# Gate and value weights of batch 0 as 16-bit parts, seven products for eight in batch 1, two score rows in one run

## The chip, the core and the metric

The kernel runs on one core of a Trainium2 chip. The metric is the time on the device in microseconds, the median of several executions. Before the change it is 1017.41 us (three executions, 1014.47 to 1018.92).

## What is computed

Three blocks in a row, with 4 batches (B), 8 heads, 576 tokens (S), head width 64. The first is causal attention plus a read of a memory, mixed by a gate for each head; the other two are feed-forward blocks. The reference, cut to the sums that matter:

```python
scores = scale * np.matmul(q, k.transpose(0, 1, 3, 2))      # then causal mask, softmax -> a
local = np.matmul(a, v)
x = g * mem_out + (1 - g) * local                            # [2304, 512]
h = (x @ w1) * (x @ w2) @ w3                                 # 512 -> 1024 -> 1024
x2 = h @ w_out                                               # 1024 -> 512
gate = 1.0 / (1.0 + np.exp(-(x2 @ w_gate)))                  # 512 -> 1536
out = gate * (x2 @ w_val) @ w_out2                           # 1536 -> 512
```

## The kernel before

**Precision.** Every product of two 32-bit matrices is made from parts: each operand is split into a high and a low part, and three matmuls (high by high, low by high, high by low) add up in PSUM (`prod`, L519). The parts are either 32-bit words of a reduced format ("fp32r" in the profile) or 16-bit words (f16). For f16 the operand is first scaled by a power of two, taken from its largest entry (`power`, L158: four one-column steps on VectorE behind a small matmul, `total`, L168, that spreads a column's sum to all partitions).

**Stages.** `ffn(b)` (L757) runs the two feed-forward blocks of batch b in four stages, with names as in the trace: `ab` (x by w1 and w2, 8 column blocks f), `xw` (h by w3 and w_out multiplied together beforehand, 4 blocks d; its result is x2), `gv` (x2 by the gate and value weights, 12 blocks f) and `ot` (by the last matrix). The matmuls have 288 columns: half of the 576 tokens (hf = 0, 1). `drive` (L1381) slips the steps of the next batch's attention in between, at the places where `ffn` yields: in ab, xw and ot, not in gv. So gv is a stage of matmuls in a row.

**Eight or seven products.** `gv` and `ab` need the products of a 2 by 2 block matrix with a 2 by 2 block matrix. In batches 0 and 1 all eight are made: 48 matmuls for a block f of gv. In batches 2 and 3 `two_rows` (L580) makes seven from sums and differences of blocks, 42 matmuls for each f, with more work behind them: adds of 288 columns on VectorE and one on GpSimd for each f. It needs the weight blocks in two forms, plain parts ("P") and parts of sums ("S", made by `sums`, L431: four adds of 256 columns on VectorE), and seven operands of x2 instead of four (`token_steps`, L546).

**Weights.** They come as 64-bit words in DRAM. `conv_step` (L379) turns half a unit (one f of gate and value is one unit, 8 blocks of 128) into 32-bit floats with two ACT steps and one DVE step, takes its largest entry (`mcol`) and stores the whole unit (`kept`). In batch 0 `split_step` (L458) then splits each half into fp32r parts, one ACT and one DVE step of 512 columns for each half, into a ring of 5 slots (`wslot`). `pump` (L489), called after each second product, does one step of each of these. The 16-bit parts are made later, by a list of tasks (`late_split`, L321): load the kept unit, split it on ACT and DVE (1024 columns), store it. A table `PACE` says at which pumps a task step comes, `limit` how far the list may go.

**Order of work.** TensorE runs in the order in which the code is written. The order on the other engines is fixed when the kernel is built, and every engine takes its instructions in that order, each waiting for its inputs. Three PSUM buffers, `f`, go round for the products and for `total`; two, `s`, hold scores. For a row block i of the scores of a head pair p, `s_part` (L1146) makes six matmuls (three for each head) and two masked reductions on DVE, which write the tiles `p`.

## Time and profile before

| what | value |
|---|---|
| median of three executions | 1017.41 us (1014.47 to 1018.92) |
| the profiled execution | 1013.13 us |
| its span in the trace | 1011.3 us |
| TensorE matmuls (PE) busy | 982.4 us, 97% |
| weight loads (PEld) busy | 797.9 us, 79% |
| VectorE (DVE) busy | 731.3 us, 72% |
| ScalarE (ACT) busy | 596.6 us, 59% |
| GpSimd (POOL) busy | 195.0 us, 19% |
| granted TensorE clock, mean | 0.995 of full speed |

The stages of the trace, found from the first and last matmul of each name: batch 0 has ab at 118 to 219 us (with the last of w3 by w_out between), xw to 257.3, gv to 334.1, ot to 385.7; batch 1 ab to 466.6, xw to 499.5, gv to 570.1, ot to 622.1; batch 2 ab to 681.5, xw to 721.3, gv to 786.0, ot to 845.0; batch 3 ab to 886.6, xw to 912.5, gv to 976.3. A busy share over the whole span says little here, since the stages differ; the table of stretches below is the one to read.

### The profile page before, as it was taken

Reading aid. Unit: us, or ns where it says so; the run is one execution under the profiler, and the core shown is the slowest. Engines: PE = TensorE matmul, PEld = TensorE weight load, DVE = VectorE, ACT = ScalarE, POOL = GpSimd, SP = SyncE. Lnnn points to the kernel's source line nnn. Section 1 sums busy time; section 2 is a strip of 40 time slices with the busy share of each in tenths; the row PEclk is TensorE's granted clock in tenths of the full one; section 3 lists DMA queues with packets and bytes.
Section 4 is the critical chain, followed back from the end, with each engine's and each line's share of the span. In section 5 each row is a group of like instructions: output and inputs, shape, how many; then the busy total and the mean of one; then the engine's idle time right before and its main releaser. Section 6 shows DMA issues by size and latency. Waiting matters only on the chain. (4 is left out here: it accounts for less than half of the span.)

```text
span 1011.3 us, 19894 instructions
## 1 busy us (share of the span) xinstructions
PE 982.4 (97%) x7351; PEld 797.9 (79%) x7351; DVE 731.3 (72%) x1702; ACT 596.6 (59%) x1213; POOL 195.0 (19%) x196
## 2 busy tenths in 40 slices
PE   7999999999999999999999999999999999999998
PEld 3556687888999898898977777778777667797776
DVE  6866788777778826777777668988876757737883
ACT  7987787567777735564654545555655545324451
POOL 3454012213000101312200011343111311201110
PEclk9989999999999999999999999999999999999999
DMA  8865799967777249877887576655655556556532
GB/s 293 245 230 192 247 346 310 326 206 254 249 250 247 98 137 380 286 226 238 297 310 261 176 251 240 214 190 184 200 181 178 185 157 204 186 174 246 183 131 79
DMA packets 95642, 227.21 MB, mean 225 GB/s; under 512 B 11192, under 2 KB 39992, under 8 KB 95288
## 3 DMA queue, kind: packets, MB, share of 16 engines
q1 hardware_dynamic: 95544, 225.93, 66.3%
q8 instruction: 58, 0.95, 0.4%
q14 instruction: 40, 0.33, 0.1%
HBM read 164.55 MB, written 61.34 MB: 223 GB/s over the span
## 5 line engine op out<-in xcount | busy, mean ns | idle before, releaser
L532 PEld LDWEIGHTS <-wslot 128*128 128x128 f16 x1680 | 162.9, 98 | 49.7 <-issue 8.3
L1200 POOL TENSOR_SCALAR p<-p,sm,omg 116x116 f32<-116x116 f32 (+4 forms) x100 | 89.0, 895 | 406.2 <-DVE sm L1198 294.9
L521 PE MATMUL gv<-x,wslot 128*128 128x288 f32 (+1 forms) x1152 | 147.5, 290 | 0.2 <-ACT gsb L137 0.2
L521 PEld LDWEIGHTS <-wslot 128*128 128x128 f16 x1152 | 111.1, 98 | 32.1 <-issue 4.5
L532 PE MATMUL gvp<-x,wslot 128*128 128x288 f16 x1008 | 125.2, 286 | 3.6 <-ACT x L180 1.6
L137 ACT ACTIVATE p<-p,sm 116x116 f32<-116x116 f32 (+4 forms) x160 | 93.2, 585 | 46.6 <-DVE sm L1174 46.5
L521 PE MATMUL ot<-hg,wslot 128*128 128x288 f16 (+1 forms) x864 | 118.1, 291 | 0.0
L521 PE MATMUL ab<-x,wslot 128*128 128x288 f32 x768 | 117.2, 302 | 0.5 <-ACT asb L800 0.3
L521 PE MATMUL xw<-h,wslot 128*128 128x288 f32 x768 | 113.0, 300 | 1.7 <-ACT h L721 1.0
L521 PEld LDWEIGHTS ab<-x,wslot 128*128 128x128 f32 x768 | 104.0, 188 | 6.3 <-issue 2.9
L521 PEld LDWEIGHTS xw<-h,wslot 128*128 128x128 f32 x768 | 103.4, 188 | 5.5 <-issue 2.0
L1174 DVE CUSTOM_DVE_ANT_0 p<-s,msk 116x116 f32<-116x116 f32 (+4 forms) x160 | 68.0, 452 | 30.8 <-PE s L1169 26.8
L532 PE MATMUL abp<-x,wslot 128*128 128x288 f16 x672 | 87.1, 286 | 1.3 <-DVE u2ab L603 1.1
L723 DVE TENSOR_TENSOR wslot<-wraw,wslot 128x512 fp32r<-128x512 f32 x76 | 54.9, 725 | 34.7 <-ACT wslot L721 34.4
L521 PEld LDWEIGHTS gv<-x,wslot 128*128 128x128 f32 x576 | 76.4, 188 | 0.5 <-ACT gsb L137 0.5
L1230 PE MATMUL t<-idf,p 116*116 116x116 f32 x480 | 68.7, 272 | 3.3 <-DVE p L1200 2.5
L1230 PEld LDWEIGHTS t<-idf,p 116*116 116x116 f32 x480 | 54.3, 139 | 18.0 <-issue 5.3
L402 ACT ACTIVATE cy<-r 128x512 f32<-128x512 f32 x76 | 51.5, 678 | 13.3 <-DVE wraw L411 2.6
L721 ACT CAST wslot<-wraw 128x512 fp32r<-128x512 f32 x76 | 47.1, 621 | 16.2 <-PE gv L521 7.4
L411 DVE SCALAR_TENSOR_TENSOR wraw<-cy,cr 128x512 int32<-128x512 int32 x76 | 54.2, 740 | 2.6 <-ACT cr L403 2.1
L521 PE MATMUL wps<-wo,wslot 128*128 128x512 f32 x192 | 52.2, 407 | 0.0
L1248 ACT COPY pt<-t 116x696 f32<-116x696 f32 (+2 forms) x74 | 47.5, 650 | 7.4 <-PE t L1230 7.1
(210 smaller groups left out, 1630.0 us busy)
## 6 DMA issues: line engine op xcount, KB each, us to landing
wslot<-k SPq DMA_DIRECT2D x40, 512.0 KB, 4.3
wslot<-ka SPq DMA_DIRECT2D x40, 512.0 KB, 4.4
wrawl<-kf SPq DMA_DIRECT2D x32, 512.0 KB, 6.1
wslot<-kb SPq DMA_DIRECT2D x40, 384.0 KB, 3.5
k<-wslot SPq DMA_DIRECT2D x24, 512.0 KB, 4.7
r<-in_gv_dram SPq DMA_DIRECT2D x24, 512.0 KB, 5.1
...
```

The costliest lines, as they stand in the source:

```text
L137: ins = nc.scalar.activation(**kw)
L402: nc.scalar.activation(out=y, in_=hi, func=AF.Prelu, scale=2.0**-112, alpha=2.0**32)
L411: nc.vector.scalar_tensor_tensor(z, y, 3, tmp["r"], ALU.logical_shift_left, ALU.bitwise_or)
L521: paced["pe"] = nc.tensor.matmul(ps, w[:, wi, blk, :], x[:, xi, cols : cols + n], start=first and part == 0, stop=last and part == 2,)
L532: paced["pe"] = nc.tensor.matmul(ps, w[:, wi, blk + k, :], x[:, xi, k, :], start=not more and k == 0 and part == 0, stop=k == 1 and part == 2,
L721: nc.scalar.copy(dst[:, 0], src)
L723: eng.tensor_sub(dst[:, 1], src, dst[:, 0].bitcast(F32))
L1174: nc.vector.tensor_tensor_reduce(out=ps_[hh][:, c0:c1], in0=os_[hh], in1=msk[:, SP - w + c0 : SP - w + c1], scale=-0.125, scalar=3.0e38 if ...
L1200: lower(SHARE_N).tensor_scalar(ps_[hh][:, :w], ps_[hh][:, :w], sm[:, 6 + hh : 7 + hh], omg[:T, 2 * p + hh : 2 * p + hh + 1], ALU.mult, ALU ...
L1230: nc.tensor.transpose(tp[:T, c : c + T], src[hh][:, j * T : (j + 1) * T], idf[:T, :T])
L1248: nc.scalar.copy(to, got)
```

## The change

In batch 0 the gate and value units are split into f16 parts at once. `scaled_step` waits until both halves of a unit are converted, makes the unit's scale (`unit_scale`: two one-column matmuls, four one-column DVE steps), splits the whole unit in one ACT and one DVE step of 1024 columns and stores the result, which batches 1 to 3 load as their "P" form. So x2 of batch 0 has to be f16 and scaled as well: its bound needs the largest entry of each h block (`htop`, 8 DVE reductions of 576 columns more) and of the product matrix (`wmax`, moved ahead into xw), and each f gets its own factor to scale back.

In batch 1 gv takes the path of batches 2 and 3 (`two_rows`, seven products), and x2 of batch 1 their `token_steps`. The task list loses its 12 "P" tasks for gate and value, and their 12 "S" tasks come first, from batch 0's ot on; the P and S tasks of a and b come after them, the S tasks of the last matrix may now run from batch 2's ab on. `PACE` is set anew.

For batches 1 to 3 the scores of row blocks 0 and 1 are made in one run of twelve matmuls, into the two `s` buffers side by side. The `p` tiles get 6 buffers instead of 5, the loads of q one instead of two.

```diff
-PB = 5
+PB = 6
-PACE = (4, 4, 4, 14, 4, 8, 4)
+PACE = (2, 9, 3, 14, 8, 5, 8)
...
-    tasks = [(u, "P") for u in jobs[:F2]] + [(("o", *x), "P") for x in pairs_of]
+    tasks = [(u, "S") for u in jobs[:F2]] + [(("o", *x), "P") for x in pairs_of]
     NFIRST = len(tasks)
     tasks += [(u, "PS") for u in jobs[F2:]]
     NPARTS = len(tasks)
-    tasks += [(u, "S") for u in jobs[:F2]]
-    NSUMS = len(tasks)
     tasks += [(("o", *x), "S") for x in pairs_of]
...
-    again = plain["ab"] + plain["xw"] + gv8 + ot8
+    again = plain["ab"] + plain["xw"] + gv16 + ot8
...
+    def unit_scale(u):
+        n = rank[u]
+        power(wsc[:, n : n + 1], wsc[:, NJ + n : NJ + n + 1], total(f"wsum{n}", *(mcol[:, hf, n : n + 1] for hf in range(2))))
+        scaled.add(u)
+    def scaled_step(u, now):
+        if ws["conv"] < 2 * u + 2:
+            return False
+        if u not in scaled:
+            if not now and ws["pumps"] < ws["ready"]:
+                return False
+            unit_scale(u)
+            return True
+        if in_use("wslot") >= RING:
+            return False
+        w = fp.tile([128, 2, 8, 128], F16, tag="wslot", name=f"wslot{ws['ring']}", bufs=RING)
+        split_scaled(w[:, 0], w[:, 1], raws.pop(u), wsc[:, rank[u] : rank[u] + 1])
+        nc.sync.dma_start(out=whole16[u]["P"], in_=w)
+        done.append((u, "P"))
+        put("wslot", [w])
+        ws["split"] += 2
+        return True
...
         if b == 2:
-            ws["pace"] = PACE[3]
+            ws["limit"], ws["pace"] = len(tasks), PACE[3]
...
-            if b > 0:
-                largest(htop[:, f : f + 1], hraw, AX.X)
+            largest(htop[:, f : f + 1], hraw, AX.X)
...
+                if b == 0 and d == 0 and n == 1:
+                    while ws["tops"] < KC:
+                        assert conv_step() or split_step()
+                    nc.vector.tensor_reduce(wmax, wtop.rearrange("p d f -> p f d"), AX.X, ALU.max)
+                    x2s = bound_x2(b, htop)
...
-            if b == 2:
+            if b:
                 for _ in two_rows(
                     take(2), x2, f"gv{b}_{f}", hraw[:, :HS], hraw[:, HS:], x2back[:, f : f + 1], True
                 ):
...
-            s = take(1 if b else 2)
+            s = take(1)
+            slot(s)
+            nc.vector.tensor_mul(x2back[:, f : f + 1], wsc[:, NJ + f : NJ + f + 1], x2s[:, 1:2])
...
         if b == 0:
             late_scales()
-            ws["limit"], ws["pace"] = F2, PACE[0]
+            ws["limit"], ws["pace"] = NFIRST, PACE[0]
...
         def s_part(p, i, n):
+            if i == 1 and not first:
+                return
+            rows = (0, 1) if i == 0 and not first else (i,)
...
+            for i, w, c0, c1, at in jobs:
+                for x, (q_, k_) in enumerate(terms):
+                    for hh in range(2):
+                        r = slice(64 * hh, 64 * hh + 64)
+                        nc.tensor.matmul(
+                            os_[hh][:, at : at + c1 - c0], q_[r, 0, i * T : (i + 1) * T], k_[r, 1, c0:c1],
+                            start=x == 0, stop=x == len(terms) - 1,
+                        )
```

How the order of instructions moves, at three places. The first is VectorE in the gv loop of batch 0, where `hgraw` is gate times value of one f, `gv0_f_hf_w` the product it reads from PSUM, `wraw` a unit being converted, `mcol` its largest entry, `wslot` its parts, and `hg` the low part of the result. Before, one whole round:

```order
L411 SCALAR_TENSOR_TENSOR wraw29_3323<-cy58_3305,cr58_3306 128x512
L411 SCALAR_TENSOR_TENSOR wraw29_3323<-cy59_3335,cr59_3336 128x512
L723 TENSOR_TENSOR wslot46_3326<-wraw27_3147,wslot46_3326 128x512
L176 TENSOR_REDUCE mcol_86<-wraw29_3323 128x1
L723 TENSOR_TENSOR hg0_0_3234<-hgraw0_0_3235,hg0_0_3234 128x576
L176 TENSOR_REDUCE mcol_86<-wraw29_3323 128x1
L964 TENSOR_TENSOR hgraw0_1_3315<-gv0_1_0_1_3343,gsb0_1_0_3341 128x288
L723 TENSOR_TENSOR wslot47_3382<-wraw27_3147,wslot47_3382 128x512
L964 TENSOR_TENSOR hgraw0_1_3315<-gv0_1_1_1_3375,gsb0_1_1_3373 128x288
```

After, half a round, from the last multiply of one f to the first of the next:

```order
L969 SCALAR_TENSOR_TENSOR hgraw0_2_3484<-gv0_2_1_1_3556,x2back0_2897,gsb0_2_1_3554 128x288
L163 TENSOR_SCALAR pw_3549<-wsum6_3546 128x1
L953 TENSOR_TENSOR x2back0_2897<-wsc_83,x2s0_2813 128x1
L164 TENSOR_SCALAR wsc_83<-pw_3549 128x1
L181 SCALAR_TENSOR_TENSOR wslot45_3530<-wraw29_3295,wsc_83,wslot45_3530 128x1024
L165 TENSOR_SCALAR pw_3549<-wsc_83 128x1
L746 TENSOR_TENSOR hg0_2_3483<-hgraw0_2_3484,hg0_2_3483 128x576
L436 SCALAR_TENSOR_TENSOR wraw32_3563<-cy64_3540,cr64_3541 128x512
L166 TENSOR_SCALAR wsc_83<-pw_3549 128x1
L436 SCALAR_TENSOR_TENSOR wraw32_3563<-cy65_3576,cr65_3577 128x512
L181 SCALAR_TENSOR_TENSOR wslot46_3566<-wraw30_3402,wsc_83,wslot46_3566 128x1024
L969 SCALAR_TENSOR_TENSOR hgraw0_3_3586<-gv0_3_0_1_3612,x2back0_2897,gsb0_3_0_3610 128x288
```

The two splits of 512 columns in each round are gone; there are splits of a whole unit (1024 columns, `wsc` is the scale) and the one-column steps of `power` (L163 to L166) and of the factor `x2back`, two units close together in every other round.

The second place is TensorE in the ab stage of batch 1, with scores of batch 2's pair 1 (`s2_1_i`). Before, row block 0, and some 40 matmuls later row block 1:

```order
L1169 MATMUL s2_1_0_0_0_5250<-qkh2_1_5194 116x116
L1169 MATMUL s2_1_0_0_1_5251<-qkh2_1_5194 116x116
L1169 MATMUL s2_1_0_0_0_5250<-qkh2_1_5194,qkl2_1_5195 116x116
L1169 MATMUL s2_1_0_0_1_5251<-qkh2_1_5194,qkl2_1_5195 116x116
L1169 MATMUL s2_1_0_0_0_5250<-qkl2_1_5195,qkh2_1_5194 116x116
L1169 MATMUL s2_1_0_0_1_5251<-qkl2_1_5195,qkh2_1_5194 116x116
L521 MATMUL ab1_3_0_1_5240<-x1_2_4327,wslot83_5064 128x288 x3
```

```order
L1169 MATMUL s2_1_1_0_0_5321<-qkh2_1_5194 116x232
L1169 MATMUL s2_1_1_0_1_5322<-qkh2_1_5194 116x232
L1169 MATMUL s2_1_1_0_0_5321<-qkh2_1_5194,qkl2_1_5195 116x232
L1169 MATMUL s2_1_1_0_1_5322<-qkh2_1_5194,qkl2_1_5195 116x232
L1169 MATMUL s2_1_1_0_0_5321<-qkl2_1_5195,qkh2_1_5194 116x232
L1169 MATMUL s2_1_1_0_1_5322<-qkl2_1_5195,qkh2_1_5194 116x232
L521 MATMUL ab1_3_1_1_5309<-x1_2_4327,wslot83_5064 128x288 x3
```

After, both stand in one run:

```order
L1181 MATMUL s2_1_1_0_0_5368<-qkh2_1_5309 116x116
L1181 MATMUL s2_1_1_0_1_5369<-qkh2_1_5309 116x116
L1181 MATMUL s2_1_1_0_0_5368<-qkh2_1_5309,qkl2_1_5310 116x116
L1181 MATMUL s2_1_1_0_1_5369<-qkh2_1_5309,qkl2_1_5310 116x116
L1181 MATMUL s2_1_1_0_0_5368<-qkl2_1_5310,qkh2_1_5309 116x116
L1181 MATMUL s2_1_1_0_1_5369<-qkl2_1_5310,qkh2_1_5309 116x116
L1181 MATMUL s2_1_1_0_0_5368<-qkh2_1_5309 116x232
L1181 MATMUL s2_1_1_0_1_5369<-qkh2_1_5309 116x232
L1181 MATMUL s2_1_1_0_0_5368<-qkh2_1_5309,qkl2_1_5310 116x232
L1181 MATMUL s2_1_1_0_1_5369<-qkh2_1_5309,qkl2_1_5310 116x232
L1181 MATMUL s2_1_1_0_0_5368<-qkl2_1_5310,qkh2_1_5309 116x232
L1181 MATMUL s2_1_1_0_1_5369<-qkl2_1_5310,qkh2_1_5309 116x232
```

One run of scores amid the products is gone for each pair of heads.

The third place is VectorE in the gv loop of batch 1, which now has the seven products (`gvp`) with their sums `u2`, `u3`. After:

```order
L631 TENSOR_TENSOR u2gv1_4_6813<-gvp1_4_6_6806,s1gv1_4_6804 128x288
L181 SCALAR_TENSOR_TENSOR wP18_6830<-wrawl_18_6534,wsc_83,wP18_6830 128x768
L181 SCALAR_TENSOR_TENSOR hg1_3_6712<-hgraw1_3_6713,hgs1_6698,hg1_3_6712 128x576
L648 TENSOR_TENSOR u3gv1_4_6842<-gvp1_4_6_6806,s1gv1_4_6804 128x288
L652 TENSOR_TENSOR u2gv1_4_6813<-gvp1_4_5_6815,u2gv1_4_6813 128x288
L659 TENSOR_TENSOR u3gv1_4_6842<-u3gv1_4_6842,gvp1_4_4_6853 128x288
L622 SCALAR_TENSOR_TENSOR hgraw1_4_6794<-s5gv1_4_6822,x2back1_6143,u2gv1_4_6813 128x288
L622 SCALAR_TENSOR_TENSOR hgraw1_4_6794<-u3gv1_4_6842,x2back1_6143,c11gv1_4_6834 128x288
L631 TENSOR_TENSOR u2gv1_5_6887<-gvp1_5_6_6880,s1gv1_5_6878 128x288
L181 SCALAR_TENSOR_TENSOR hg1_4_6793<-hgraw1_4_6794,hgs1_6698,hg1_4_6793 128x576
```

A split of a task (`wP18`, 768 columns, of a and b) stands between the adds that free PSUM buffers; 16 instructions of tasks stand in this stage in all, 8 splits and 8 adds of 256 columns, and in that of batch 2 before the change there were 5.

## Rows read from the trace of the kernel before

**Rows 1.** The page, busy time of each engine with its share of the span.

```profile
PE 982.4 (97%) x7351; PEld 797.9 (79%) x7351; DVE 731.3 (72%) x1702; ACT 596.6 (59%) x1213; POOL 195.0 (19%) x196
```

**Rows 2.** Stretches: PE, PEld, DVE, ACT, POOL busy (instructions), clock, DMA.

```profile
118.00:219.00 101.00, 97.89 (x698) 83.33 (x697) 80.23 (x189) 69.72 (x152) 18.05 (x17) 1.00 0.88 307
219.00:257.30 38.30, 36.64 (x285) 32.59 (x284) 30.66 (x75) 26.79 (x58) 9.86 (x8) 1.00 0.75 261
257.30:334.10 76.80, 76.56 (x578) 76.26 (x578) 60.36 (x108) 58.25 (x110) 0.00 (x0) 1.00 0.72 244
...
499.50:570.10 70.60, 70.60 (x580) 56.40 (x579) 51.95 (x90) 39.23 (x55) 0.00 (x0) 1.00 0.80 270
...
622.10:681.50 59.40, 58.17 (x480) 43.25 (x478) 52.96 (x147) 34.18 (x85) 24.31 (x23) 1.00 0.69 225
...
721.30:786.00 64.70, 62.59 (x507) 49.30 (x506) 49.65 (x103) 33.97 (x64) 9.41 (x12) 1.00 0.57 192
786.00:845.00 59.00, 56.75 (x465) 41.09 (x464) 43.07 (x108) 32.18 (x61) 10.30 (x10) 1.00 0.51 163
...
912.50:976.30 63.80, 62.33 (x507) 49.24 (x506) 48.97 (x103) 31.45 (x63) 9.40 (x12) 1.00 0.56 195
```

**Rows 3.** PE in order of time, gate and value products of batch 0.

```profile
262.42 71.82 PE L521 MATMUL gv<-x,wslot 128*128 128x288 f32 x540 [0.24 <-ACT gsb L137]
334.09 0.21 PE L172 MATMUL wsum<-mcol,ones 128*128 128x20 bf16 x2
334.15 1.85 PE L521 MATMUL ot<-hg,wslot 128*128 128x288 f32 x12
```

**Rows 4.** PE in order of time, the same products in batches 1 and 2.

```profile
517.18 53.08 PE L521 MATMUL gv<-x,wslot 128*128 128x288 f16 x432
...
743.41 42.79 PE L532 MATMUL gvp<-x,wslot 128*128 128x288 f16 x348 [0.31 <-ACT s5gv L608]
```

**Rows 5.** DVE in order of time, one round of batch 0's gate and value loop.

```profile
283.42 0.45 DVE L964 TENSOR_TENSOR hgraw<-gv,gsb 128x288 f32<-128x288 f32 x1
283.79 1.28 DVE L411 SCALAR_TENSOR_TENSOR wraw<-cy,cr 128x512 int32<-128x512 int32 x2
284.99 0.68 DVE L723 TENSOR_TENSOR wslot<-wraw,wslot 128x512 fp32r<-128x512 f32 x1
285.59 0.68 DVE L176 TENSOR_REDUCE mcol<-wraw 128x1 bf16<-128x512 f32 x1
286.19 0.75 DVE L723 TENSOR_TENSOR hg<-hgraw,hg 128x576 fp32r<-128x576 f32 x1
286.86 0.68 DVE L176 TENSOR_REDUCE mcol<-wraw 128x1 bf16<-128x512 f32 x1
287.45 0.45 DVE L964 TENSOR_TENSOR hgraw<-gv,gsb 128x288 f32<-128x288 f32 x1
289.17 0.69 DVE L723 TENSOR_TENSOR wslot<-wraw,wslot 128x512 fp32r<-128x512 f32 x1 [1.27 <-ACT wslot L721]
289.78 0.45 DVE L964 TENSOR_TENSOR hgraw<-gv,gsb 128x288 f32<-128x288 f32 x1
```

**Rows 6.** PE in order of time, a run of scores amid batch 1's products.

```profile
410.83 5.41 PE L521 MATMUL ab<-x,wslot 128*128 128x288 f32 x39
416.17 0.31 PE L1169 MATMUL s<-qkh 64*116 64x116 f32 x2
...
416.62 0.66 PE L521 MATMUL ab<-x,wslot 128*128 128x288 f32 x3
417.11 0.76 PE L1230 MATMUL t<-idf,p 116*116 116x116 f32 x6
```

**Rows 7.** Groups by shape: busy us, mean ns | idle before, releaser.

```profile
L176 DVE TENSOR_REDUCE htop<-hraw 128x1 f32<-128x576 f32 x24 | 17.9, 747 | 0.4
...
L181 DVE SCALAR_TENSOR_TENSOR wP<-wrawl,wsc,wP 128x1024 f16<-128x1024 f32 x12 | 15.7, 1305 | 11.6 <-ACT wP L180 11.0 <-DMA wslot<-k 0.5
...
L1198 DVE RECIPROCAL sm<-sm 116x2 f32<-116x2 f32 x80 | 12.8, 160 | 1.3
```

More of the change, by code (lines that the diff above doesn't have):

```diff
@@ L271, in tile_attention_memory_ffn @@
     wot = {}
-    ws = {"conv": 0, "step": 0, "split": 0, "ring": 0, "freed": 0, "use": 0, "again": 0, "pumps": 0, "late": 0, "task": 0, "part": 0, "limit": 0, "pace": 0, "tops": 0, "wo": 0, "pass": 0, "wready": False}
+    ws = {"conv": 0, "step": 0, "split": 0, "ring": 0, "freed": 0, "use": 0, "again": 0, "pumps": 0, "late": 0, "task": 0, "part": 0, "limit": 0, "pace": 0, "ready": 0, "tops": 0, "wo": 0, "pass": 0, "wready": False}
     tmp = {}
+    scaled = set()
     last = {}
@@ L327, in late_split @@
         late_o2 = u not in rank
+        if late_o2 and "o2" not in scaled:
+            scaled.add("o2")
+            o2_scale()
+            return
         by = o2s[:, 0:1] if late_o2 else wsc[:, rank[u] : rank[u] + 1]
@@ L464, in split_step @@
         u, hf = divmod(s, 2)
+        if u in rank and rank[u] < F2:
+            return scaled_step(u, now)
         r = raws[u][:, 4 * hf : 4 * hf + 4, :]
@@ L870, in measure @@
         def measure(f):
[L871 to L877 removed]
+            if f == 0:
                 for n, m in enumerate((0, 1, 5, 4)):
@@ L1173, in s_part @@
[L1173 to L1183 removed]
+            if i == 1 and not first:
+                return
@@ new lines, in s_part @@
+            rows = (0, 1) if i == 0 and not first else (i,)
+            jobs = []
+            at = 0
+            for i in rows:
+                w = T * (i + 1)
+                if n == 0:
+                    ps_ = []
+                    for hh in range(2):
+                        name = f"p{b}_{p}_{i}_{hh}"
+                        if first and np_["n"] % 2 == 0:
+                            m = np_["n"] // 2 % P0
+                            ps_.append(fp.tile([T, 2 * S], F32, tag=f"h{m}", name=name, bufs=1)[:, :SP])
+                        else:
+                            ps_.append(ap.tile([T, SP], F32, tag="p", name=name, bufs=PB))
+                        np_["n"] += 1
+                    sp[p, i] = (ps_, ap.tile([T, 8], F32, tag="sm", name=f"sm{b}_{p}_{i}", bufs=6))
+                c0, c1 = (0, w) if w <= 512 else ((0, SP // 2), (SP // 2, SP))[n]
+                jobs.append((i, w, c0, c1, at))
+                at += c1 - c0
@@ new lines, in s_part @@
+            os_ = [
+                ps_s.tile([128, 512], F32, tag="s", name=f"s{b}_{p}_{i}_{n}_{hh}")[:T, :at] for hh in range(2)
+            ]
+            terms = [(qks[p], qks[p])] if first else [(parts[p][x], parts[p][y]) for x, y in ((0, 0), (1, 0), (0, 1))]
+            for i, w, c0, c1, at in jobs:
+                for x, (q_, k_) in enumerate(terms):
+                    for hh in range(2):
+                        r = slice(64 * hh, 64 * hh + 64)
+                        nc.tensor.matmul(
+                            os_[hh][:, at : at + c1 - c0], q_[r, 0, i * T : (i + 1) * T], k_[r, 1, c0:c1],
+                            start=x == 0, stop=x == len(terms) - 1,
+                        )
```

133 lines of the change are left out of this document (39 added, 94 removed).

## The prediction

> **What bounds the kernel now.** I read the page first: matmuls keep TensorE busy for 982.4 us of the span [rows 1], so the kernel ends when TensorE has done its list, and the change is worth what it takes off that list, less the new waits. A share over the whole span hides the stages, so the table of stretches came next [rows 2]. In gv of batch 0 TensorE is busy 76.56 of 76.80 us and weight loads 76.26; in gv of batch 1, with f16 parts, 70.60 of 70.60 and loads 56.40. Neither has waits worth naming: only a shorter list helps. VectorE is the engine to watch, since the new work lands on it: 60.36 of 76.80 there, and 52.96 of 59.40 in ab of batch 2, the fullest stretch shown. Then TensorE in order of time gave the price of one product [rows 3, 4, 6], and VectorE in order of time the room that is left in a round [rows 5]. The granted clock is 1.00 in all these stretches, the 2.4 GHz level.
>
> The profiled execution took 1013.13 us with a span of 1011.3; the median shown is 1017.41, 4.3 us more. I make the sum as a difference and take it off the median.
>
> **Gate and value of batch 0.** 540 fp32r matmuls take 71.82 us, 133.0 ns each [rows 3]; f16 ones 53.08 us for 432, 122.9 ns [rows 4]. For 576 that is 10.1 ns x 576 = 5.8 us off. Added are 24 one-column matmuls in 12 pairs; the nearest row is `wsum`, a pair after which the next product starts 0.06 us later [rows 3]: 12 x 0.06 = 0.7 us, if their operands are there. They are: by the order, each unit's `mcol` steps stand well ahead of its pair.
>
> What can spoil this is VectorE. Its round for one f takes 6.36 us now (283.42 to 289.78), of which it sits idle 1.27 us for ScalarE's part of the split [rows 5]. By starts, two conversions take 1.20 us, a largest entry 0.60, `hg` 0.67, a multiply 0.37 to 0.45. After: two conversions 1.20, two largest 1.20, one split of 1024 columns 1.22 (the row has 1.305 [rows 7]; neighbours overlap by about 0.08), two multiplies 0.88, `hg` 0.67, and five one-column steps, which no row shows alone: between 0.04 and 0.16 us each (the two-column reciprocal [rows 7]); I take 0.1, since other steps stand between them. Sum 5.7 us, from 5.4 to 6.0. TensorE's round becomes 48 x 0.1229 + 0.06 = 5.96 us. So VectorE just keeps up on average, but not evenly: the order puts two splits, two conversions, `hg` and the small steps between one multiply and the next, 5.3 us, while TensorE makes the next product in 24 x 0.1229 = 2.95 us. The multiply then comes 2.3 us late, and what waits behind it is the product that needs its PSUM buffer: with three buffers about 2.95 us of lateness cost nothing, with a `total` in between about half. I take 2.0 us of waits over the 8 or 9 full rounds; the ends are 0 and the case where the idle 1.27 us stays in each round (second rival). Another 0.3 us goes where gv begins, since the last split of x2 stands behind conversions and unit splits; the ends are 0 and the 1.66 us that TensorE now idles in xw (38.30 less 36.64 [rows 2]). Net gain 5.8 - 0.7 - 0.3 - 2.0 = **2.8 us**.
>
> ScalarE costs nothing: 24 casts of 512 columns become 12 of 1024, and it is busy 58.25 of 76.80 us [rows 2]. Of the DMAs, the 12 late loads and 12 late stores of the P tasks go, and 12 stores come into gv. Such a store waits in SyncE's queue for its split, and behind it stand the loads of the next raw halves; these run three halves ahead, a round and a half or 8.9 us, which covers it. Without that cover conversion would wait, as in the second rival.
>
> **Gate and value of batch 1.** The stage takes 70.60 us; the same stage with seven products takes 64.70 in batch 2 and 63.80 in batch 3 [rows 2]. These hold the waits at the start for the seven operands, the GpSimd adds and the extra DVE work; the products run at 42.79 us for 348, 123.0 ns [rows 4]. But batch 1 also has tasks in it: 16 VectorE instructions, some 13 us (8 splits at 1.0 to 1.3 us, 8 short adds at about 0.44), against 5 of some 3 us in batch 2. VectorE would be busy 49.65 + 10 = 60 of 65 us. The nearest row for that is ab of batch 2, 52.96 of 59.40 us with the same seven products and tasks, where TensorE idles 1.23 us [rows 2]. I take 64.70 + 1.6 = 66.3: gain **4.3 us**, from 6.8 (as batch 3) to -4 (each task's work exposed).
>
> The Trainium skill, "Perfetto Trace Analysis", section "Identifying the Most-Contended Engine", says that matmul busy time does not tell how far TensorE is from its limit, that the busy share of LDWEIGHTS does, and that for VectorE occupancy is a fair measure. By it TensorE would have room in f16 stages (loads busy 56.40 of 70.60 us), and ab of batch 2 would be VectorE's stage (89% against 73%). The trace does not agree: TensorE idles there 1.23 us in 59.40, and f16 products come every 122.9 ns however busy the loads are. By the page the stage limit of gv in both batches would be VectorE's load, about 60 us and with the waits the second rival's time.
>
> **Scores.** Twelve runs go (three batches, four pairs). Three ab matmuls after a run take 0.49 us to the next foreign matmul; at the rate of the long stretch, 5.34 us for 39, they would take 0.41 [rows 6]. So a break costs about 0.1 us on entering, and the run of six (0.45 us) holds about as much for leaving. One break less: 0.15 us x 12 = **1.8 us**, from 1.0 to 2.4. The same reductions stand on VectorE, and both `s` buffers stay taken a little longer; row block 2's scores come later than either.
>
> **Tasks moved.** In ot of batch 2 TensorE idles 59.00 - 56.75 = 2.25 us and VectorE is busy 43.07 us with the last tasks in it [rows 2]; the order has none there after. Gain **1.0 us**, from 0 to 2.25. Five or six of them now lie in gv of batch 2: loss 0.5 us, up to 1.5.
>
> **Costs elsewhere.** Eight largest entries of h at 0.747 us [rows 7] are 6.0 us more on VectorE in ab of batch 0, where it is busy 80.23 of 101 us and TensorE idles 3.1 [rows 2]: 1.0 us more idle (0 to 3). The last of them stands ahead of the last split of h, for which TensorE already waits: 0.7 us. In batch 1's ab the S tasks come at every fifth pump: 0.5 us; in ot of batch 0, where they replace the P tasks, 0.2. Together with 0.5 above: **2.9 us**.
>
> **Sum.** 2.8 + 4.3 + 1.8 + 1.0 - 2.9 = 7.0 us. 1017.4 - 7.0 = **1010.4 us**, 0.7% less.
>
> **Rivals.**
> First, everything is hidden: VectorE keeps up in both gv stages. Then 5.8 - 0.7 = 5.1 from batch 0, 6.8 from batch 1, 2.4 from scores, 1.5 from ot and no costs: 15.8 us, 1001.6. For it: TensorE hardly waits at 89% VectorE load [rows 2]. Against: the uneven order in batch 0.
>
> Second, slower: VectorE and ScalarE wait for each other in gv of batch 0 as they do now, and the 1.27 us stay [rows 5]. The round becomes 6.0 + 1.27 = 7.3 us instead of 6.36, and nine rounds lose 8.5 us instead of gaining 2.8: 1010.4 + 11.3 = 1021.7. The whole change turns slower than before where the round passes 6.36 + (7.0 - 2.8) / 9 = 6.8 us, that is with 1.1 us of idle time in a round of 5.7. Against it: the split now waits for a scale made pumps earlier and is needed later, as a slot holds a whole unit and five units fit the ring instead of two and a half.
>
> Third, batch 1's tasks are exposed: the splits stand between the adds that free PSUM buffers, and 10 us more VectorE work lengthen the stage to 74.7 us: 4.1 lost instead of 4.3 won, 1018.8. Half of it gives 1014.6. For it: products of 0.74 us and three buffers leave little room. Against: ab of batch 2.
>
> Fourth, the order on the engines as built differs in stages that the edits don't name, and eats the gain: 1015.
>
> **Chances.** Forecast 0.52 (1006 to 1014.5), first rival 0.20, second 0.09, third 0.13, fourth 0.06. The range leaves out the lower half of the first rival and most of the second: **1001.5 to 1018.5**. About 0.5%, 5.1 us, is what a measurement of this kernel can tell from no change. Faster by more (under 1012.3): 0.42 of the forecast, all of the first, little else: 0.62. Slower by more (over 1022.5): half of the second and a little of the third: 0.08. Within: 0.30.
>
> **What would show it.** In the trace after: gv of batch 0 in about 73.5 us with products 122.9 ns apart, and TensorE's waits there naming `hgraw` or `wsum`; gv of batch 1 in about 66.3 us; 24 `wsum` matmuls without waits; VectorE idle in ot of batch 2; one run of twelve score matmuls in each pair. The prediction is wrong if VectorE's round in batch 0's gv takes over 6.4 us, if gv of batch 1 takes over 68 us, or if TensorE's idle time grows by more than 3 us in ab of batch 0.

## The result and the profile after

The changed kernel takes **1029.29 us** (median of four executions, 1026.71 to 1032.05), against 1016.28 before (four executions): a ratio of 1.0133, with a 95% interval of 1.0098 to 1.0168. It is 13 us slower where 7 us less were forecast. The profiled execution took 1032.05 us with a span of 1030.3, 18.9 more than that of before, so a sum over stages of the two traces comes to more than the medians' 13: the traced execution of before is one of the fast ones of its kernel, the one after the slowest of four.

The page after, busy time of each engine, to be held against [rows 1]:

```profile
PE 976.5 (95%) x7303; PEld 776.8 (75%) x7303; DVE 763.0 (74%) x1804; ACT 597.9 (58%) x1220; POOL 207.5 (20%) x208
```

TensorE's list did get shorter, by 5.9 us of busy time, yet the span is 19 us longer. So it waits more: span less busy time was 28.9 us and is 53.8. Where, the table of stretches after tells, with the columns of [rows 2]: ab, xw and gv of batch 0, ab and gv of batch 1, ab, gv and ot of batch 2.

```profile
119.50:228.90 109.40, 100.15 (x698) 85.61 (x697) 84.02 (x190) 69.60 (x151) 17.64 (x15) 0.97 0.81 282
228.90:271.50 42.60, 39.48 (x290) 35.05 (x291) 35.07 (x98) 29.25 (x59) 9.48 (x8) 0.92 0.75 264
271.50:347.90 76.40, 72.03 (x597) 56.80 (x595) 67.33 (x147) 60.91 (x102) 0.00 (x0) 1.00 0.87 318
...
397.30:484.50 87.20, 81.49 (x624) 71.94 (x624) 74.04 (x186) 46.56 (x106) 21.32 (x20) 0.96 0.72 248
...
518.00:585.30 67.30, 63.06 (x508) 49.20 (x505) 56.71 (x113) 38.58 (x71) 10.51 (x12) 1.00 0.83 284
...
637.20:701.30 64.10, 58.75 (x481) 43.34 (x480) 56.95 (x147) 35.36 (x87) 24.36 (x23) 1.00 0.61 199
...
741.80:807.10 65.30, 62.82 (x508) 49.37 (x508) 52.92 (x112) 35.06 (x66) 10.16 (x12) 1.00 0.60 193
807.10:864.40 57.30, 55.51 (x464) 40.94 (x462) 27.89 (x79) 27.14 (x56) 10.23 (x9) 1.00 0.27 79
```

The stages that the change rewrites, gv of batch 0 and 1 and ot of batch 2, are shorter. The loss lies in ab of batch 0 (+8.4), xw of batch 0 (+4.1), ab of batch 1 (+6.4) and ab of batch 2 (+4.6). In three of the four the granted clock is below 1.00, where it was 1.00 before. The row of before for ab of batch 1:

```profile
385.70:466.60 80.90, 80.19 (x626) 70.32 (x625) 59.98 (x160) 48.97 (x108) 22.12 (x20) 1.00 0.81 283
```

TensorE in order of time, the longest waits in ab and xw of batch 0 and ab of batch 1 after the change:

```profile
129.46 1.41 PE L1244 MATMUL t<-idf,p 116*116 116x116 f32 x6 [2.74 <-DVE p L1214]
160.09 0.61 PE L1244 MATMUL t<-idf,p 116*116 116x116 f32 x2 [3.32 <-DVE p L1214]
205.52 0.38 PE L1244 MATMUL t<-idf,p 116*116 116x116 f32 x2 [2.19 <-DVE p L1214]
234.45 0.53 PE L549 MATMUL xw<-h,wslot 128*128 128x288 f32 x2 [1.54 <-ACT h L744]
236.35 0.61 PE L549 MATMUL xw<-h,wslot 128*128 128x288 f32 x1 [1.37 <-DVE h L746]
406.48 0.66 PE L1244 MATMUL t<-idf,p 116*116 116x116 f32 x2 [4.90 <-DVE sm L1212]
```

The first is a run of transposes `t` of row block 2, which waited 0.76 us before. Three are transposes of row block 0 of a head pair; before, none of these waited over 0.6 us. What delays these three stands on VectorE. Before, from the reductions of row block 0 to its `p`, the pair that begins at 146.7 us:

```profile
149.06 0.27 DVE L1174 CUSTOM_DVE_ANT_0 p<-s,msk 116x116 f32<-116x116 f32 x1
...
149.45 0.75 DVE L723 TENSOR_TENSOR h<-hraw,h 128x576 fp32r<-128x576 f32 x1
150.12 1.21 DVE L176 TENSOR_REDUCE mcol<-wraw 128x1 bf16<-128x1024 f32 x1
151.81 0.17 DVE L1197 TENSOR_SCALAR sm<-sm 116x2 f32<-116x2 f32 x1 [0.48 <-ACT p L137]
...
152.22 0.34 DVE L1200 TENSOR_SCALAR p<-p,sm,omg 116x116 f32<-116x116 f32 x1
```

After, the same pair (scores at 149.9 us):

```profile
150.85 0.74 DVE L176 TENSOR_REDUCE htop<-hraw 128x1 f32<-128x576 f32 x1
...
152.78 0.27 DVE L1188 CUSTOM_DVE_ANT_0 p<-s,msk 116x116 f32<-116x116 f32 x1
...
153.18 1.22 DVE L176 TENSOR_REDUCE mcol<-wraw 128x1 bf16<-128x1024 f32 x1
154.31 0.39 DVE L1188 CUSTOM_DVE_ANT_0 p<-s,msk 116x232 f32<-116x232 f32 x1
...
155.61 0.82 DVE L1114 SCALAR_TENSOR_TENSOR mphi<-qnr,me 116x640 f32<-116x640 f32 x1
156.35 0.68 DVE L746 TENSOR_TENSOR wslot<-wraw,wslot 128x512 fp32r<-128x512 f32 x1
156.95 0.15 DVE L1212 RECIPROCAL sm<-sm 116x2 f32<-116x2 f32 x1
157.03 1.42 DVE L1211 TENSOR_SCALAR sm<-sm 116x2 f32<-116x2 f32 x1
158.36 1.28 DVE L436 SCALAR_TENSOR_TENSOR wraw<-cy,cr 128x512 int32<-128x512 int32 x2
159.57 0.38 DVE L1214 TENSOR_SCALAR p<-p,sm,omg 116x116 f32<-116x116 f32 x1
```

From the first reduction to `p` it was 3.2 us and is 6.8. VectorE is never idle in between: its order has a reduction of a weight unit, row block 1's reductions, the memory read (`mphi`), a split and two conversions ahead of the one short step that TensorE needs. The largest entry `htop` stands ahead of all this, and the first reduction starts 2.9 us behind the first score matmul, where it was 2.3. The wait of 4.90 us in ab of batch 1 has the same form, with the steps of S tasks in the chain (`wS` is a split; a sum of 1.61 us at 404.27, shown in the last section, is another):

```profile
399.23 0.27 DVE L1188 CUSTOM_DVE_ANT_0 p<-s,msk 116x116 f32<-116x116 f32 x1
...
401.56 1.28 DVE L181 SCALAR_TENSOR_TENSOR wS<-wrawl,wsc,wS 128x1024 f16<-128x1024 f32 x1
...
405.88 0.14 DVE L1211 TENSOR_SCALAR sm<-sm 116x2 f32<-116x2 f32 x1
```

### The profile page after: what moved, and what is told of

Its sections match the earlier page's. It is cut to its first block, busy times and chain, and to the rows that moved or that the text cites. A ratio compares the mean times of both kernels' runs of the same rounds, so it can differ in the third digit from the quotient of the medians.

```text
span 1030.3 us, 19908 instructions
## 1 busy us (share of the span) xinstructions
PE 976.5 (95%) x7303; PEld 776.8 (75%) x7303; DVE 763.0 (74%) x1804; ACT 597.9 (58%) x1220; POOL 207.5 (20%) x208
## 4 chain that ended last, share of the span: by engine, by line
PE 63%; DVE 16%; DMA 11%; ACT 6%; issue 3%; POOL 0%; SPq 0%; DVEq 0%; ACTq 0%; POOLq 0%
PE gvp L560 14%; PE xw L549 8%; PE ot L549 8%; PE ab L549 6%; PE abp L560 5%; PE s L1181 5%; PE o L1312 4%; PE t L1244 3%; PE gv L549 3%; PE wps L549 2%; DMA wraw<-wd 2%; DVE p L1188 2%; DMA wslot<-kb 2%; PE o L1297 2%; DMA wd<-wpart 2%
## 5 line engine op out<-in xcount | busy, mean ns | idle before, releaser
L560 PEld LDWEIGHTS <-wslot 128*128 128x128 f16 x2184 | 212.1, 98 | 73.0 <-issue 18.9
L560 PE MATMUL gvp<-x,wslot 128*128 128x288 f16 x1512 | 188.6, 286 | 8.0 <-ACT x L180 3.4
L549 PEld LDWEIGHTS <-wslot 128*128 128x128 f16 x1152 | 110.5, 98 | 36.0 <-issue 8.7
L549 PE MATMUL ab<-x,wslot 128*128 128x288 f32 x768 | 119.4, 307 | 0.3 <-DVE hraw L824 0.3
L137 ACT ACTIVATE p<-p,sm 116x116 f32<-116x116 f32 (+4 forms) x160 | 93.1, 584 | 41.0 <-DVE sm L1188 40.7
L549 PEld LDWEIGHTS ab<-x,wslot 128*128 128x128 f32 x768 | 107.5, 194 | 5.6 <-issue 3.2
L1188 DVE CUSTOM_DVE_ANT_0 p<-s,msk 116x116 f32<-116x116 f32 (+4 forms) x160 | 66.9, 453 | 33.9 <-PE s L1181 33.8
L549 PE MATMUL gv<-x,wslot 128*128 128x288 f16 x576 | 72.0, 286 | 3.7 <-ACT gsb L137 3.7
L653 POOL TENSOR_TENSOR s5gv<-u3gv,s5gv 128x288 f32<-128x288 f32 x36 | 30.6, 851 | 200.7 <-DVE u3gv L648 187.2
L746 DVE TENSOR_TENSOR wslot<-wraw,wslot 128x512 fp32r<-128x512 f32 x52 | 38.1, 733 | 24.2 <-ACT wslot L744 24.0
L1312 PE MATMUL o<-pt,vs 116*64 116x344 f32 (+2 forms) x320 | 50.7, 424 | 0.0
```

The source lines that it names most:

```text
L137: ins = nc.scalar.activation(**kw)
L549: paced["pe"] = nc.tensor.matmul(ps, w[:, wi, blk, :], x[:, xi, cols : cols + n], start=first and part == 0, stop=last and part == 2,)
L560: paced["pe"] = nc.tensor.matmul(ps, w[:, wi, blk + k, :], x[:, xi, k, :], start=not more and k == 0 and part == 0, stop=k == 1 and part == 2,
L746: eng.tensor_sub(dst[:, 1], src, dst[:, 0].bitcast(F32))
L1188: nc.vector.tensor_tensor_reduce(out=ps_[hh][:, c0:c1], in0=os_[hh][:, at : at + c1 - c0], in1=msk[:, SP - w + c0 : SP - w + c1], scale=-0 ...
L1312: nc.tensor.matmul(ot[r, XO + q0 : XO + S], v_[:, j, hh], pt[:, hh, j].rearrange("p a c -> p (a c)")[:, q0 - X : S - X] if j < 4 else pt[: ...
```

## Experiments

Lengths of the stages in the traces, us, from first matmul to first matmul (ab0 is ab of batch 0, and so on; "rest" is all else in the span), and each kernel's median. A "ratio" below is that to the kernel before, with a 95% interval; the edits are shown in their main lines, with `...` where lines are left out:

| kernel | ab0 | xw0 | gv0 | ab1 | gv1 | ab2 | rest | median |
|---|---|---|---|---|---|---|---|---|
| before | 101.2 | 38.2 | 76.9 | 80.8 | 70.6 | 59.4 | 584.2 | 1015.5 to 1017.2 |
| changed | 109.6 | 42.3 | 76.4 | 87.2 | 67.3 | 64.0 | 583.5 | 1029.3 |
| `rows_apart` | 100.5 | 42.5 | 75.6 | 86.5 | 68.0 | 61.2 | 584.8 | 1022.5 |
| `rows_only` | 102.2 | 41.4 | 76.9 | 80.0 | 70.6 | 62.7 | 583.2 | 1017.2 |
| `less_vector` | 101.9 | 41.6 | 77.4 | 80.2 | 69.1 | 63.9 | 581.0 | 1017.3 |
| `apart_own_bank` | 101.5 | 40.3 | 74.4 | 85.9 | 68.0 | 61.2 | 585.0 | 1019.3 |
| `apart_bank_hold` | 100.9 | 42.6 | 73.8 | 80.8 | 69.7 | 61.2 | 586.7 | 1015.0 |
| `apart_bank_top` | 100.4 | 42.5 | 74.8 | 82.1 | 69.7 | 61.2 | 582.0 | 1013.8 |
| `eight_b1` | 101.2 | 42.0 | 76.0 | 79.7 | 70.6 | 59.4 | 585.3 | 1017.1 |
| `after_hold` | 107.6 | 42.8 | 76.2 | 82.8 | 74.1 | 63.9 | 582.5 | 1030.9 |
| `bank_hold_order` | 100.5 | 40.7 | 74.3 | 79.9 | 68.0 | 61.2 | 585.8 | 1011.9 |
| `bank_hold_clear` | 100.9 | 39.0 | 74.0 | 81.8 | 66.0 | 63.1 | 583.4 | 1010.9 |
| `clear_pace3` | 101.5 | 38.7 | 74.5 | 87.0 | 65.0 | 63.6 | 583.3 | 1017.5 |
| `clear_merged` | 111.0 | 40.7 | 73.2 | 85.4 | 66.9 | 66.7 | 576.3 | 1024.6 |

(The time ahead of ab0 varies from 113.5 to 122.4 us between traces; it is part of "rest". There is one trace for each kernel. A stage whose code is the same in several kernels differs by up to 2.3 us between their traces: ab1 from 79.9 to 82.1 in runs 5, 6, 9 and 10, xw0 40.3 and 42.6 in runs 4 and 5. So a difference of that size in one stage is not resolved.)

**1. `rows_apart`**: `s_part` as before the change, in the changed kernel (main lines; the loads of q get their two buffers back too).

```diff
-PB = 6
+PB = 5
-            rows = (0, 1) if i == 0 and not first else (i,)
+            rows = (i,)
```

> The changed kernel with its score part undone: row blocks 0 and 1 of the scores each in their own run, 5 p tiles and two q loads as before the change; all else as changed. Theory A (the merged run is what costs: the transposes of row block 0 wait for a chain that now has the reductions of row block 1 in it, 3.3, 2.2, 4.9 and 0.8 us in ab of batches 0 and 1, and the clock falls to 0.50 behind two of these waits, about 4.6 us more; the merge itself saves 1.8): those waits vanish, ab of batch 0 takes 102 to 104 us and of batch 1 81 us, the whole about 1015 us. Theory B (VectorE has too much work: largest entries of h in batch 0, sums of weight blocks in batch 1; the merge is harmless): the waits at transposes stay within 3 us of their sum, the whole takes 1029 to 1031 us.

Measured 1022.47, ratio 1.0063 (1.0042 to 1.0084). Ab of batch 0 is back at 100.5, so the merge is needed for that loss; ab of batch 1 is not. Neither theory holds for the whole. In this run and in runs 2 and 12 "the merge" is the one run of scores together with 6 `p` tiles and one buffer for the loads of q; no run takes these apart.

**2. `rows_only`**: the reverse, the merge alone in the kernel before.

```diff
-PB = 5
+PB = 6
-            rows = (i,)
+            rows = (0, 1) if i == 0 and not first else (i,)
```

> The kernel before with the score part of the change alone: row blocks 0 and 1 in one run of twelve matmuls, 6 p tiles, one q load. Theory A (the merged run costs): slower than before by 6 to 14 us, 1022 to 1030 us, with waits of over 2 us at transposes of row block 0. Theory B (VectorE's new work costs, the merge is harmless): 1.8 us faster than before, about 1014.5 us, no wait over 1.5 us at these transposes.

Measured 1017.19, ratio 1.0007 (0.9983 to 1.0032): no difference. Neither theory holds: no transpose of row block 0 waits over 2 us, though one run of row block 2 does (2.40 us, at 129.09), and the 1.8 us are not won. The two traces do not show how it balances, since that of before is 5.7 us shorter although the medians agree: there the losses (ab2 +3.3, xw0 +3.2, ab0 +1.0) are larger than the gains (ab1, xw1, ot stages). In xw0 the granted clock is 0.92, for 1.00 in the trace of before.

**3. `less_vector`**

```diff
-            largest(htop[:, f : f + 1], hraw, AX.X)
+            if b > 0:
+                largest(htop[:, f : f + 1], hraw, AX.X)
+            elif f == 0:
+                nc.vector.memset(htop, 1.0)
...
-            sums(raw, nc.vector, nc.vector)
+            if u not in rank or rank[u] >= F2:
+                sums(raw, nc.vector, nc.vector)
```

> The changed kernel, scores merged, without the VectorE work that the change put into ab of batch 0 and 1: it leaves out the largest entries of h in batch 0 (a constant stands for them) and the four sums of weight blocks in each S task of gate and value (the parts are made of the plain blocks). Theory A (the merged run costs by itself): the waits at transposes of row block 0 stay, over 5 us in ab of batch 0 and 1 together, the whole takes 1021 us or more. Theory B (VectorE's load costs): these waits are under 2 us in all, ab of batch 0 takes 102 us and of batch 1 80 us, the whole about 1014 us.

Measured 1017.31, 12 below the changed kernel; ab0 and ab1 go back to 101.9 and 80.2 although the scores are merged. With runs 1 and 2: in ab of batch 0 **either** half alone is nearly free, the merge (102.2) and the largest entries (100.5), and both together cost 8 us. In ab of batch 1 the loss goes with the sums while the scores stay merged (87.2 to 80.2), and it is there without the merge as well (run 1, 86.5).

**4. `apart_own_bank`**: `rows_apart` and

```diff
+        own = name[:4] == "wsum" and len(name) > 4
-        ps = ps_f.tile([128, 512], F32, tag="f", name=name)
+        ps = (ps_s if own else ps_f).tile([128, 512], F32, tag="s" if own else "f", name=name)
```

> The kernel of rows_apart, and besides the 12 pairs of one-column matmuls that give a unit's scale write to the PSUM buffers of the scores (idle in gv of batch 0) instead of taking one of the three that the products use. Theory C (gv of batch 0 lost its gain because such a buffer is held until VectorE reads the sum, near 3 us, and the products go on with two): gv of batch 0 takes 72.5 to 74 us instead of 76.4, the whole 2.5 to 4 us less than rows_apart. Theory D (VectorE and ScalarE are late by themselves): gv of batch 0 stays within 1 us of 76.4, the whole within 1.5 us of rows_apart.

Measured 1019.33; gv0 goes from 75.6 us in `rows_apart` to 74.4. The spans of the two traces differ by 2.8 us, but 2.2 of that are in xw0, where the clock did not fall this time. A pair of traces gives 1.2 us, then, between the two theories; all traces give more: the seven kernels with this edit have gv0 at 73.2 to 74.8, mean 74.1, the five others with f16 weights in batch 0 at 75.6 to 77.4, mean 76.3. The held buffer costs 2.2 us, near the lower end of theory C (2.4 us off 76.4). The changed kernel's rows (TensorE, then VectorE) show the buffer held for 3.0 us, from the first `wsum` to its reader, while the products go on with two:

```profile
308.28 0.19 PE L172 MATMUL wsum<-mcol,ones 128*128 128x1 bf16 x2
310.11 1.63 PE L549 MATMUL gv<-x,wslot 128*128 128x288 f16 x12 [1.65 <-ACT gsb L137]
```

```profile
308.95 0.75 DVE L746 TENSOR_TENSOR hg<-hgraw,hg 128x576 fp32r<-128x576 f32 x1
...
311.24 0.15 DVE L163 TENSOR_SCALAR pw<-wsum 128x1 int32<-128x1 int32 x1
```

**5. `apart_bank_hold`**: `apart_own_bank` and

```diff
-            ws["limit"], ws["pace"] = NFIRST, PACE[0]
+            ws["limit"], ws["pace"] = 3, PACE[0]
...
-        if b == 1:
-            ws["limit"], ws["pace"] = NFIRST, PACE[5]
...
+            if b == 1 and f == 1:
+                ws["limit"], ws["pace"] = NFIRST, 4
```

> The kernel of apart_own_bank with the S tasks of gate and value held back at the seam of batch 0 and batch 1: three of them in ot of batch 0, none in the first block f of ab of batch 1, from the second block on one step at every fourth pump. Their number is the same. Theory E (only the place costs: sums and splits that stand between the first row blocks' softmax steps at the head of ab of batch 1, waits of 1.09 and 2.60 us in rows_apart and the fallen clock behind them): ab of batch 1 takes 80.5 to 82 us instead of 85.8, the whole 1014.5 to 1015.5 us instead of 1019.3. Theory F (VectorE has too much work in the whole stage): ab of batch 1 stays over 84.5 us, the waits turn up later in it, and the whole stays within 1.5 us of 1019.3.

Measured 1015.01, ab1 80.8: as theory E forecast. The stage still holds the same 7 splits `wS`, and 28 of the 31 sums that it held in run 4, so it is mostly the place that changed and a little the amount. VectorE is busy 65.2 us in it instead of 70.9: the three sums are 1.3 us of that, and most of the rest is that only 3 instructions, no longer 8, take far longer than usual beside GpSimd, as the last section tells. In `rows_apart` the crowd at the head of that stage is two splits `wS` amid the second row block's steps (VectorE, then the wait on TensorE):

```profile
395.25 2.28 DVE L181 SCALAR_TENSOR_TENSOR wS<-wrawl,wsc,wS 128x1024 f16<-128x1024 f32 x1
...
398.87 1.27 DVE L181 SCALAR_TENSOR_TENSOR wS<-wrawl,wsc,wS 128x1024 f16<-128x1024 f32 x1
```

```profile
402.22 1.00 PE L1234 MATMUL t<-idf,p 116*116 116x116 f32 x4 [2.60 <-DVE mn L1121]
```

In this trace gv1 is 1.7 us longer than in run 4. That is not held work coming back: the stage has the same tasks in both, and the waits of 1.54 and 1.80 us for x2 at its head stand in both. It is the granted clock, 0.98 instead of 1.00, with TensorE busy 1.7 us longer for the same matmuls (`apart_own_bank`, then `apart_bank_hold`):

```profile
506.80:574.80 68.00, 63.03 (x507) 49.20 (x507) 57.61 (x113) 38.58 (x70) 11.19 (x13) 1.00 0.80 274
```

```profile
504.10:573.80 69.70, 64.73 (x507) 50.04 (x506) 57.66 (x113) 38.65 (x70) 11.23 (x13) 0.98 0.79 276
```

**6. `apart_bank_top`**: `apart_bank_hold`, the last largest entry written later.

```diff
+            if b or f < F1 - 1:
-            largest(htop[:, f : f + 1], hraw, AX.X)
+                largest(htop[:, f : f + 1], hraw, AX.X)
...
+                    largest(htop[:, F1 - 1 : F1], hraw, AX.X)
                     nc.vector.tensor_reduce(wmax, ...)
```

> The kernel of apart_bank_hold, and the last of the eight largest entries of h in batch 0 is taken after the first half of xw's first block instead of right behind the last block of ab. Theory G (this reduction of 0.74 us stands before the last split of h on VectorE, makes the second wait at the head of xw 1.37 us instead of 0.70, and with it the clock falls to 0.50 for some 6 us in most executions): that wait is 0.7 to 0.8 us, the clock stays at 1.00, xw of batch 0 takes 38.5 to 39.5 us, and the whole is 1 to 3 us below apart_bank_hold. Theory H (the wait is that of the split itself): no change in xw of batch 0, the whole within 1 us of apart_bank_hold.

Measured 1013.77, not resolved from run 5, the wait still 1.36 us. This tests nothing: VectorE's order came out the same, the reduction still ahead of the split.

```profile
223.13 0.73 DVE L177 TENSOR_REDUCE htop<-hraw 128x1 f32<-128x576 f32 x1
...
224.54 0.74 DVE L747 TENSOR_TENSOR h<-hraw,h 128x576 fp32r<-128x576 f32 x1
```

**7. `eight_b1`**: `rows_apart` with batch 1 of before.

```diff
-    tasks = [(u, "S") for u in jobs[:F2]] + [(("o", *x), "P") for x in pairs_of]
+    tasks = [(("o", *x), "P") for x in pairs_of]
...
+    tasks += [(u, "S") for u in jobs[:F2]]
...
-            if b:
+            if b > 1:
                 for _ in two_rows(
```

> The kernel of rows_apart with batch 1 as before the change: eight products for each block of gate and value, the S tasks of gate and value behind those of a and b, the table of paces of before. What is left of the change is f16 gate and value weights in batch 0. If the seven products of batch 1 with their earlier S tasks are the larger loss: 1016 to 1018 us (gv of batch 0 75.6 us, ab of batch 1 near 80, gv of batch 1 70.6), 5 us below rows_apart. If the f16 weights of batch 0 themselves bring the loss of rows_apart: 1020 us or more.

Measured 1017.07, ratio 1.0014 (0.9993 to 1.0035), as the first theory says. The f16 weights of batch 0, made as the change makes them (the held buffer of run 4 included), are worth nothing that can be resolved; seven products in batch 1 with their earlier S tasks, as the change schedules them, lose 5.4 us.

**8. `after_hold`**: the edit of run 5 in the changed kernel.

> The changed kernel, scores merged, with only the hold of apart_bank_hold in it. Theory E (place of the S tasks at the head of ab of batch 1): ab of batch 1 takes 81 to 82 us instead of 87.2, the whole about 1023.5 us instead of 1029.3, and ab of batch 0 keeps its 109 us. Theory F (VectorE's load in the whole stage): ab of batch 1 over 85 us, the whole over 1027 us.

Measured 1030.85. Ab1 falls from 87.2 to 82.8, nearly as theory E says, but the time does not: gv1 grows from 67.3 to 74.1. Of these 6.8 us TensorE's busy time makes 4.4, at a granted clock of 0.93 in the stage, and longer waits 2.4, one of them 3.12 us at its head for the operands of x2. Ahead of these operands VectorE stood idle for a load of q, which has one buffer in this kernel:

```profile
507.43 0.49 DVE L1111 TENSOR_SCALAR me<-qnr 116x640 f32<-116x640 f32 x1 [2.96 <-DMA qnr<-in_qn_dram]
```

From ab0 on, VectorE waits for q loads in all five kernels with one such buffer (0.7 and 0.8 us in the changed kernel, up to 2.34 us in `clear_merged`), and in none of the nine with two. What the single buffer costs by itself no run tests.

**9. `bank_hold_order`**: `apart_bank_hold`, and a dependency that fixes the order.

```diff
+            paced["h"] = split_rows(ht, hraw, SHARE_H)
+            top = largest(htop[:, f : f + 1], hraw, AX.X)
+            if b == 0 and f == F1 - 1:
+                behind(top, "h")
```

> The kernel of apart_bank_hold, and on VectorE the last largest entry of h in batch 0 now stands behind the last split of h (a dependency in the order alone; apart_bank_top, which only wrote it later, left it 0.73 us ahead of the split). Theory G: the second wait at the head of xw of batch 0 falls from 1.37 to 0.65 to 0.75 us; if the clock then stays at 1.00, xw takes 38.5 to 39.5 us instead of 42.6, if it still falls, 41.5; the whole 0.7 to 3 us below apart_bank_hold (1015.0). Theory H (the wait is that of the split itself): the wait stays over 1.2 us, no change.

Measured 1011.86, ratio 0.9945 (0.9923 to 0.9966). The wait is 0.70, as before the change:

```profile
228.45 0.40 PE L550 MATMUL xw<-h,wslot 128*128 128x288 f32 x1 [0.70 <-DVE h L747]
```

This is theory G for the wait. In this trace the clock still fell there (xw0 40.7); in `bank_hold_clear` it did not (39.0). That the longer wait is what makes the clock fall is not shown: it fell in `rows_only`, where this wait is 0.71 us, and not in `apart_own_bank`, where it is 1.37.

**10. `bank_hold_clear`**

```diff
+            if b == 1 and d == KC - 1:
+                ws["pace"] = 0
...
-        if b == 1:
-            ws["limit"], ws["pace"] = NPARTS, PACE[1]
...
+            if b == 1 and f == 1:
+                ws["limit"], ws["pace"] = NPARTS, PACE[1]
```

> The kernel of bank_hold_order with no task step in the last block of xw and the first block of gv of batch 1. In apart_bank_hold the S tasks that were taken from the head of ab came back at the head of gv: waits of 1.54 and 1.80 us for operands of x2, gv of batch 1 69.7 us instead of 68.0. If a task's steps stand ahead of these operands: waits there under 1 us each, gv of batch 1 67 to 68 us, the whole 1.5 to 2.5 us below bank_hold_order. If the operands are late by their own chain: no change within 1 us; if the tasks then come too late for their loads, gv of batch 1 grows to over 70.5.

Measured **1010.91, ratio 0.9936 (0.9915 to 0.9957)**: faster than both kernels, though not resolved from `bank_hold_order`. Gv1 takes 66.0, with waits under 0.8 us at its head, as the first theory says; the waits it removes were not those of the hold, since `apart_own_bank` has them too (run 5). Ab1 and ab2 are 1.9 us longer. In ab1 the tasks are the same, and 1.9 us are within the spread between traces; ab2 now holds 18 task instructions on VectorE instead of 12.

**11. `clear_pace3`**: the 4 of run 5 becomes 3.

> The kernel of bank_hold_clear with the task steps of ab and xw of batch 1 at every third pump instead of every fourth, so that the S tasks are done earlier and fewer are left for gv. If VectorE has room in ab of batch 1: ab stays at 80.5 to 81.5 us, gv of batch 1 67 us, the whole 0 to 1.5 us below bank_hold_clear. If the sums crowd the softmax steps as in the changed kernel: ab over 83 us, the whole 2 us or more above bank_hold_clear.

Measured 1017.47. Ab1 is 87.0, with a wait of 3.59 us at a transpose: one step more in every twelve pumps brings the whole loss of that stage back. It holds 9 splits and 36 sums now, for 7 and 28, so here the amount changed as well as the place.

**12. `clear_merged`**: `bank_hold_clear` with the merge.

> The kernel of bank_hold_clear (1010.9 us) with the scores of row blocks 0 and 1 merged again as in the change, with its 6 p tiles and one q load: all other losses found so far are out of the way. If the merged run costs because it lengthens the chain ahead of the first transposes on a VectorE that now also takes the largest entries of h: ab of batch 0 takes 107 to 109 us instead of 100.9 with waits of 2 to 3.3 us at transposes of row block 0, ab of batch 2 near 64 us, the whole 1017 to 1022 us. If its cost in the changed kernel came from the other parts: the whole 1009 to 1011 us, by the 1.8 us of twelve runs saved.

Measured 1024.61, ratio 1.009 (1.0057 to 1.0124): 13.7 us more than `bank_hold_clear` for the merge alone, more than forecast. Ab0 is 111.0, with the wait of 3.3 us back:

```profile
157.25 0.61 PE L1249 MATMUL t<-idf,p 116*116 116x116 f32 x2 [3.29 <-DVE p L1219]
```

## Why the prediction was wrong

**Gate and value of batch 0** (2.8 forecast). TensorE's busy time fell by 4.5 us (5.8 less 0.7 forecast), and 4.4 us of waits, 0.2 before, took it back: 0.5 won. The mechanism was named, "with a `total` in between about half", but its price of 2.3 us (2.0 and 0.3) was too low: the held buffer costs 2.2 us alone (run 4), and kernels without it stand at 73.2 to 74.8 us, where 73.5 to 74 was forecast. The second rival did not happen: a round takes 76.4 / 12 = 6.4 us, under its 6.8.

**Gate and value of batch 1** (4.3 forecast). 3.3 measured, 67.3 us against 66.3: right within its bounds. The third rival, tasks exposed in that stage, did not happen.

**Scores** (1.8 forecast). The saving is there: a run of twelve costs 0.82 us to the next product, two of six cost 0.45 and 0.52. The failing step is the sentence that "the same reductions stand on VectorE". They do, but ahead of row block 0's `sm` and `p`, for which TensorE waits at a fixed place of its order, some 4 to 7 us behind the scores. With `htop` also there, that costs 8 us in ab of batch 0 (runs 1, 3, 12); in ab of batch 2 the merge costs 3 us (run 2). The order view that was read was TensorE's; it was VectorE's that decided.

**Tasks moved** (1.0 forecast): ot of batch 2 is 1.6 us shorter, and gv of batch 2 is 0.5 us longer, as forecast.

**Costs elsewhere** (2.9 forecast). This is the term that failed most: the four stages lost 8.4 + 4.1 + 6.4 + 4.6 = 23.5 us in the traces, some 11 of them with the merge (above). "In batch 1's ab the S tasks come at every fifth pump: 0.5 us" was 6. I priced VectorE work by its share of a stage (room left, idle time) and not by what it stands in front of. Ab of batch 1 has VectorE busy 74.0 of 87.2 us, a smaller share than ab of batch 2 before with 1.2 us of waits, and run 5 takes the loss away with the same splits and nearly all sums. The 0.7 us for the last largest entry of h ahead of its split was right (0.67, run 9); the rest of xw's 4.1 us is mostly the clock. It fell in that stage in `rows_only` and `less_vector` too, which have no such entry, and the trace of before is one in which it did not; so that part is not shown to come from the change.

The rule of the Trainium skill, "Perfetto Trace Analysis", section "Identifying the Most-Contended Engine", set aside in the prediction, would now name VectorE in ab of batch 1 (busy 85%, weight loads 82%), as it did in ab of batch 2 before (89% and 73%). The traces agree for the first stage and not for the second, where TensorE idled only 1.2 us: an occupancy says nothing of place.

**The clock** was no term of the sum at all. Behind the wait of 4.90 us the granted clock is 0.50, the 1.2 GHz level, for some 7 us (changed kernel, columns as in [rows 2]):

```profile
404.00:406.00 2.00, 0.00 (x0) 0.00 (x0) 2.00 (x5) 0.09 (x1) 1.53 (x1) 0.94 1.03 412
406.00:408.00 2.00, 1.52 (x7) 1.48 (x8) 1.89 (x7) 1.42 (x2) 1.12 (x2) 0.50 1.03 415
408.00:410.00 2.00, 2.00 (x10) 2.00 (x10) 1.97 (x4) 0.00 (x0) 0.00 (x0) 0.50 0.71 275
410.00:412.00 2.00, 2.00 (x11) 1.32 (x9) 0.22 (x2) 0.40 (x1) 0.00 (x0) 0.50 0.61 178
412.00:414.00 2.00, 2.00 (x14) 2.00 (x15) 1.65 (x6) 1.49 (x5) 0.00 (x0) 0.86 1.00 340
```

TensorE's busy time is 2.3, 2.8 and 1.3 us longer in ab0, xw0 and ab1 than before with no more to do (seven one-column matmuls in xw0 apart). In ab0 the clock fell behind the waits of 2.74 and 3.32 us, for some 3 us each. So of the 23.5 us some 17 are waits and 6 are matmuls at the lower clock.

**Rivals.** The first, everything hidden, did not happen either. The fourth, an order on the engines that differs in stages that the edits don't name, comes nearest to what happened, with a chance of 0.06 and a price of 1015: VectorE's order decided, but in ab of batch 0 and 1, too, which the edits do name, and its size was not right. The sign given for being wrong, over 3 us more idle time in ab of batch 0, came true (3.1 to 9.3 us).

What stays open: how much of the cost in ab2 (1.8 us without the merge, none in `eight_b1`) is due to which task; the stage holds 10 task instructions on VectorE in `eight_b1` (59.4 us), 12 in `rows_apart` (61.2) and 18 in `bank_hold_clear` (63.1). Open, too, is why `clear_merged` loses 3.6 us in ab of batch 1, where `rows_only` gains. There VectorE is busy 70.3 us for 65.2 with the same 182 instructions, and stands idle 1.46 and 2.34 us for q loads, which points at the single buffer; no run tests it.
